# Queueing weight splits and head preparation behind the gates, and taking two experts' maxima from raw weights

## The chip, the cores and the metric

One core of a Trainium2 chip runs the kernel in one launch. The metric is device time in microseconds: the median of the timed runs, and beside it one execution taken by the hardware profiler. The engines named below are TensorE (PE, with its weight loads as PEld), VectorE (DVE), ScalarE (ACT), GpSimd (POOL) and SyncE (SP), whose queue issues all DMAs.

## The reference

Attention with a decay over 4 batches, 8 heads, 576 positions and 64 columns a head; its output is the input of four experts whose outputs are added with normalised weights. All of it is float32.

```python
def _attn_ref(q, k, v, f):
    scores = scale * np.matmul(q, k.transpose(0, 1, 3, 2))
    cum = np.cumsum(np.log(np.clip(f, 0.0001, 1.0)), axis=-1)
    decay = cum[:, :, :, None] - cum[:, :, None, :]
    scores = np.where(causal, -1000000000.0, scores + decay)
    scores = scores - np.max(scores, axis=-1, keepdims=True)
    attn = np.exp(scores)
    attn = attn / (np.sum(attn, axis=-1, keepdims=True) + 1e-09)
    return np.matmul(attn, v)

def _moe_ref(x, domain_probs, w1, w2):      # x: 2304 x 512; w1: 4 x 512 x 1024
    p = domain_probs / (domain_probs.sum(-1, keepdims=True) + 1e-09)
    for e in range(E):
        h = np.maximum(x @ w1[e], 0.0)
        out += p[:, e:e + 1] * (h @ w2[e])
```

## The kernel before

Every float32 product is made of several products of shorter numbers: an operand is split into a high part and the low rest (`hi` and `kl` of a head's q and k, `wh` and `wl` of weights, `gh` and `gl` of the hidden layer), and three of the four combinations are added up in PSUM.

The 2304 tokens are nine chunks of 256. Chunks 0 to 3 are the first 256 positions of each batch (half 0 of the heads), the others the remaining 320 (half 1). After a startup that runs the heads of batch 0, half 0, the experts begin while attention goes on.

The experts' work is a list of 80 **steps**. Weights come in 64 **units** (`w[n % 32]`: 128 hidden columns of `w1` and of `w2`, 512 KB); units 0 to 31 are sweep 0, with chunks 0 to 2 at fp32r, and units 32 to 63 sweep 1, the same weights at f16 for chunks up to 4. A step takes one chunk through two units: `l1` (24 products, L1010), the gate (`gh` by ScalarE at L1023, kept as `self.first`; `gl` by VectorE at L1024, `self.last`), and `l2` (12 products, L1043) with a drain into `acc` (L1070). Step n traces `l1` of n, its gate, then `l2` of n - 1. Chunks 5 to 8 follow in a last stage (from about 630 us, `Big` and `Second`) that reads the split weights back from DRAM (`wd`).

Between these calls `pace` traces attention's work, which the list `asteps` orders and whose costs set how much goes into each quarter step. For head n `head_steps` traces: `prep_v` and `prep` of the next head (`prep_hi`: `hi` on ScalarE L562, `q` on GpSimd L563; `prep_lo`: `kl` L571 and the low rows of `hi` L577 on GpSimd), the loads of the head after that, the score products (L615), minima (L629), exponentials (L644), for half 1 the f16 pair `z` (L713, L714) that a transposing DMA turns into `pt` (L723).

`w_split(n)` is traced at the end of the step whose unit it replaces, six units ahead. In sweep 0 it makes `wh` on ScalarE (L950) and `wl` in two halves (L954), on GpSimd from unit 16 on. In sweep 1 it scales by `wsc`: the first half by ScalarE (L977) and VectorE (L978), the second by GpSimd (L969), ScalarE (L972) and GpSimd (L973); two steps later a DMA writes the pair to `wd`. Raw weights lie in three buffers `wr`, loaded up to three units ahead.

The scale `wsc` of an expert needs the maxima of all its weights ahead of sweep 1. `w_peek` loads each expert's units once more in 16 halves (`pk`, 256 KB, L281), one a step from the step in `PEEK` on, and reduces them two steps later (L284); `w_scale` follows 17 steps after the start and sends the maxima through DRAM (`tops`).

What order the engines' queues have is not that of the text. A scheduler draws it up ahead of time, in a timeline of its own: an instruction may go into its engine's queue ahead of others traced before it, when its data and its buffer are there sooner. On the chip each queue then runs strictly in that order. `tc.issue_after(i)` adds an edge of order alone: what the block traces on i's engine is queued behind i. The helper `behind` uses it with the last step's `gl`.

Of the kernel before, what the change touches and what calls it, by code (L numbers as in the profile page):

```python
# [29 lines left out]
WIDE = (0, 1, 2)  # L30
PEEK = (1, 15, 31, 45)
V_PEEK = 1
# [5 lines left out]
EARLY = (54, 58)  # L38
AHEAD = 4
W_SLOT = (4, 6)  # L40
NEAR = 2
# [37 lines left out]
def fused(ctx: ExitStack, tc: tile.TileContext, qk, v, f, probs, w, out):  # L79
# [413 lines left out]
    class Job:  # L493
# [71 lines left out]
        def prep_lo(self, hh):  # L565
            if hh not in self.kl:
                self.rows(hh)
            wq, wk, ko, qo = self.wq, self.wk, self.ko, self.qo
            r, hi, kl = self.raw[hh], self.hi[hh], self.kl[hh]
            eng = nc.vector if self is jobs[0] else nc.gpsimd  # L570
            eng.tensor_tensor(  # L571
                out=kl[:64, :wk],
                in0=r[:64, ko : ko + wk],
                in1=hi[:64, ko : ko + wk].bitcast(F32),
                op=ALU.subtract,
            )
            eng.tensor_tensor(  # L577
                out=hi[64:128, qo : qo + wq],
                in0=r[64:128, qo : qo + wq],
                in1=hi[64:128, qo : qo + wq].bitcast(F32),  # L580
                op=ALU.subtract,
            )

        def prep(self, hh):
# [291 lines left out]

    zs, pts = [], []
    jobs = []
# [6 lines left out]
    def head_steps(n):  # L885

        st = []
        if FIRST < n < len(heads) and heads[n][1] == 0:
            st.append((0, heads[n][0].prep_v))
        if n + 1 < len(heads):  # L890
            j, hh = heads[n + 1]
            st.append((0, lambda j=j, hh=hh: j.prep(hh)))
        if n + 2 < len(heads):
# [50 lines left out]
    def w_split(n):  # L944
        w_load(n)
        r = wraw.pop(n)
        if n < 32:
            wh[n] = w_p.tile([128, 1024], F32R, tag="wh", name=f"wh{n}")
            wl[n] = w_p.tile([128, 1024], F32R, tag="wl", name=f"wl{n}")
            nc.scalar.activation(out=wh[n], in_=r, func=AF.Copy)  # L950
            eng = nc.vector if n in W_DVE else nc.gpsimd
            for a in (0, 512):
# [664 lines left out]

    used = set()
    for n in range(len(steps) + 1):
# [4 lines left out]
        for e, first_ in enumerate(PEEK):  # L1624
            if 0 <= n - first_ < 16:
                w_peek(e, n - first_)
            if n == first_ + 17:
                a_, b_ = w_scale(e)
                behind(a_)
                at_step(n + 3, b_)  # L1630
        if 0 <= n - V_PEEK < NV:
# [29 lines left out]
        if prev is not None:  # L1661
# [6 lines left out]
            for w0, t in ends.items():  # L1668
                if t is prev:
                    if w0 + 7 < NS:  # L1670
                        w_split(w0 + 6)
                        w_split(w0 + 7)
                    first_units(w0)
        prev = cur

# [89 lines left out]
```

## Time and profile before

| what | us |
|---|---|
| median of 3 runs | 936.33 (935.25 to 938.32) |
| profiled execution | 940.96 |
| its span, first to last instruction | 939.2 |
| TensorE busy | 884.8 |
| VectorE busy | 718.5 |
| ScalarE busy | 567.5 |
| GpSimd busy | 523.7 |

Busy time is the union of an engine's instructions. A value in square brackets behind a row of the timeline is the idle time of the engine before it and what ended it. Times are counted from the span's start.

### The profile page before, as it was taken

How to read it: one execution, taken by the hardware profiler on the slowest of the kernel's cores; microseconds unless marked ns; L12 is line 12 of the kernel's file. 1: busy time of each engine (PE TensorE's matmuls, PEld its weight loads, DVE VectorE, ACT ScalarE, POOL GpSimd, SP SyncE). 2: the span in 40 equal slices, each digit the busy share in tenths (PEclk: the TensorE clock that was granted, in tenths of full speed). 3: DMA queues.
4: the chain of work that ended last, by engine and by line, in shares of the span. 5: the costliest groups of instructions: out<-in, count | busy, mean ns of one | idle time of the engine just before them, and what ended most of it. 6: DMA issues, size and time to landing. Idle time of an engine off the chain costs nothing.

```text
span 939.2 us, 16651 instructions
## 1 busy us (share of the span) xinstructions
PE 884.8 (94%) x5783; PEld 618.9 (66%) x5783; DVE 718.5 (77%) x1458; ACT 567.5 (60%) x1137; POOL 523.7 (56%) x528
## 2 busy tenths in 40 slices
PE   4899999999988999899899999999998999999998
PEld 3699998998755656676566656654455664566547
DVE  5768777786899988789887777576768756786487
ACT  5869766465577667567766676355665345653350
POOL 4666866567533564227752674165778627785060
PEclk9689999999989999999999999999999999999999
DMA  7458855647889799977999698514322423232003
GB/s 263 147 166 308 273 139 172 199 134 235 258 245 184 161 298 217 251 160 160 327 289 183 138 304 219 141 58 146 131 91 79 149 68 120 83 106 75 23 1 91
DMA packets 147508, 159.45 MB, mean 170 GB/s; under 512 B 86148, under 2 KB 107328, under 8 KB 147424
## 3 DMA queue, kind: packets, MB, share of 16 engines
q1 hardware_dynamic: 147424, 158.39, 60.8%
q8 instruction: 45, 0.74, 0.3%
q14 instruction: 39, 0.32, 0.1%
HBM read 117.30 MB, written 21.65 MB: 148 GB/s over the span
## 4 chain that ended last, share of the span: by engine, by line
PE 23%; POOL 13%; DVE 6%; ACT 5%; issue 4%; DMA 2%; POOLq 0%; DVEq 0%; ACTq 0%
PE y L1281 6%; PE m L1281 5%; PE l L1043 5%; POOL s L1341 5%; PE l L1010 4%; POOL wt L1175 4%; POOL wu L1175 2%; DMA wr<-in_w 2%; POOL bs L1207 1%; PE s L615 1%; DVE acc L1070 1%; POOL wr L969 1%; PE o L815 1%; DVE rl L1162 1%; ACT wt L1202 1%
## 5 line engine op out<-in xcount | busy, mean ns | idle before, releaser
L1010 PE MATMUL l<-y,w 128*128 128x256 f16 x1248 | 154.7, 273 | 1.1 <-DVE gl L1024 1.1
L644 ACT ACTIVATE p<-p,nm 128x576 f32<-128x576 f32 (+3 forms) x160 | 95.6, 598 | 72.9 <-DVE nm L629 63.4
L1010 PEld LDWEIGHTS <-w 128*128 128x128 f16 x1248 | 117.7, 98 | 33.3 <-issue 8.9
L1043 PE MATMUL l<-w,gh 128*128 128x512 f16 x408 | 125.1, 390 | 6.9 <-DVE acc L1070 5.3
L714 DVE SCALAR_TENSOR_TENSOR z<-p,rs,z 128x384 f16<-128x384 f32 (+3 forms) x128 | 92.0, 743 | 9.3 <-ACT z L713 7.3
L615 PE MATMUL s<-hi 128*128 128x384 f32 (+1 forms) x192 | 75.5, 397 | 20.6 <-DVE hi L577 8.8
L563 POOL CAST q<-raw 64x320 fp32r<-64x320 f32 (+1 forms) x56 | 26.6, 476 | 120.0 <-PE s L615 79.5
L1070 DVE SCALAR_TENSOR_TENSOR acc<-y,scg,acc 128x256 f32<-128x256 f32 (+1 forms) x164 | 81.1, 515 | 14.9 <-PE y L1281 14.7
L571 POOL TENSOR_TENSOR kl<-raw,hi 64x576 fp32r<-64x576 f32 (+1 forms) x56 | 65.3, 1166 | 39.4 <-ACT hi L562 38.6
L1281 PE MATMUL m<-rh,bs 128*128 128x512 f16 x256 | 86.4, 379 | 0.0
L629 DVE CUSTOM_DVE_ANT_0 p<-s,mask 128x288 f32<-128x288 f32 (+2 forms) x160 | 74.7, 474 | 13.1 <-PE s L615 12.4
L1207 POOL TENSOR_TENSOR bs<-wt,bs 128x512 f16<-128x512 f32 x32 | 38.4, 1202 | 78.2 <-ACT bs L1206 78.0
L1043 PE MATMUL l<-w,gl 128*128 128x512 f16 x204 | 78.5, 390 | 2.0 <-DVE gl L1024 2.0
L969 POOL TENSOR_SCALAR wr<-wr,wsc 128x512 f32<-128x512 f32 x32 | 54.5, 1708 | 36.5 <-DMA wr<-in_w 36.0
L713 ACT ACTIVATE z<-p,rs 128x384 f16<-128x384 f32 (+3 forms) x128 | 69.5, 589 | 6.6 <-DVE rs L675 4.5
L954 POOL TENSOR_TENSOR wl<-wr,wh 128x512 fp32r<-128x512 f32 x48 | 63.1, 1339 | 12.5 <-ACT wh L950 6.9
L1010 PE MATMUL l<-xh,wh 128*128 128x256 f32 x224 | 66.5, 299 | 0.8 <-ACT xh L856 0.8
L1043 PEld LDWEIGHTS <-gh 128*128 128x128 f16 x408 | 37.2, 100 | 44.6 <-issue 14.2
L1024 DVE SCALAR_TENSOR_TENSOR gl<-l,gh 128x512 f16<-128x512 f32 (+1 forms) x80 | 54.7, 684 | 15.0 <-ACT gh L1023 14.4
L1010 PE MATMUL l<-xl,wh 128*128 128x256 f32 x224 | 66.2, 295 | 0.0
L1010 PE MATMUL l<-xh,wl 128*128 128x256 f32 x224 | 65.7, 293 | 0.1
L1281 PE MATMUL m<-rh,bw 128*128 128x512 f16 x191 | 64.4, 379 | 1.4 <-ACT r L1327 1.4
(385 smaller groups left out, 2349.0 us busy)
## 6 DMA issues: line engine op xcount, KB each, us to landing
wr<-in_w SPq DMA_DIRECT2D x90, 512.0 KB
pk<-in_w SPq DMA_DIRECT2D x64, 256.0 KB
wd<-w SPq DMA_DIRECT2D x32, 512.0 KB
raw<-in_qk SPq DMA_DIRECT2D x32, 448.0 KB
bw<-wd SPq DMA_DIRECT2D x32, 256.0 KB
bv<-wd SPq DMA_DIRECT2D x32, 256.0 KB
raw<-in_qk SPq DMA_DIRECT2D x24, 256.0 KB
vp<-in_v SPq DMA_DIRECT2D x10, 512.0 KB
```

Source lines behind the costliest of these rows:

```text
L571: eng.tensor_tensor(out=kl[:64, :wk], in0=r[:64, ko : ko + wk], in1=hi[:64, ko : ko + wk].bitcast(F32), op=ALU.subtract,)
L615: nc.tensor.matmul(out=ps[:, at : at + z - a], lhsT=lhsT, rhs=rhs, start=(m == 0), stop=(m == 1),)
L629: nc.vector.tensor_tensor_reduce(out=pt[:, a:z], in0=ps, in1=mask[:, m0 + a : m0 + z], scale=-0.125, scalar=BIG if n == 0 else nm[:, col : ...
L644: nc.scalar.activation(out=pt[:, :w_], in_=pt[:, :w_], func=AF.Exp, scale=-1.0, bias=self.nmax[hh][:, c : c + 1], accum_out=self.ssum[:, h ...
L713: nc.scalar.activation(out=o[:, 0], in_=x, func=AF.Copy, scale=sc)
L714: nc.vector.scalar_tensor_tensor(out=o[:, 1], in0=x, scalar=sc, in1=o[:, 0], op0=ALU.mult, op1=ALU.subtract)
L954: eng.tensor_tensor(out=wl[n][:, a:z], in0=r[:, a:z], in1=wh[n][:, a:z].bitcast(F32), op=ALU.subtract,)
L969: nc.gpsimd.tensor_scalar(out=r[:, c], in0=r[:, c], scalar1=sc, scalar2=None, op0=ALU.mult)
L1010: nc.tensor.matmul(out=self.l1p[:, fi, :], lhsT=lhsT, rhs=rhs[:, k, :], start=(k == 0 and m == 0), stop=(k == 3 and m == 2),)
L1043: matmul(out=l2[tt], lhsT=lhsT, rhs=rhs, start=(self.ps == 0 and fi == 0 and m == 0), stop=(self.ps == 1 and fi == 1 and m == 2),)
L1070: nc.vector.scalar_tensor_tensor(out=acc[c][:, tt, d0:d1], in0=ps, scalar=sc, in1=acc[c][:, tt, d0:d1], op0=ALU.mult, op1=ALU.add,)
L1281: line.append(nc.tensor.matmul(**args))
```

## The change

Four things change.

- `w_split` is traced inside `paced`, which queues its ScalarE part behind the step's `gh`, its VectorE part behind that step's `gl`, and its GpSimd part behind the last low rows of a head (`lows[-1]`, L577) that were traced so far. The pairs of units that follow a step with `ps` 1 are traced `REST` steps later, by the number of chunks in the sweep.
- `prep` and `prep_v` of the next head are traced inside `held`, the same with the step before.
- Only experts 0 and 1 are still loaded in halves for their maxima. Those of experts 2 and 3 are reduced in `w_split` of units 16 to 31, from the raw unit that lies there, by one reduction over 2 x 512 columns.
- `w_scale` follows at the steps of `SCALE`: 18 and 32 as before for experts 0 and 1, 37 and 42 for 2 and 3 (48 and 62 before).

```diff
-PEEK = (1, 15, 31, 45)
+PEEK = (1, 15)
+SCALE = (18, 32, 37, 42)
+REST = (0, 0, 1, 2, 3)
@@ prep_lo
-            eng.tensor_tensor(
+            i = eng.tensor_tensor(
                 out=hi[64:128, qo : qo + wq],
...
+            if self is not jobs[0]:
+                lows.append(i)
@@ head_steps
-            st.append((0, heads[n][0].prep_v))
+            st.append((0, lambda j=heads[n][0]: held(j.prep_v)))
-            st.append((0, lambda j=j, hh=hh: j.prep(hh)))
+            st.append((0, lambda j=j, hh=hh: held(lambda: j.prep(hh))))
@@ w_split, units below 32
             nc.scalar.activation(out=wh[n], in_=r, func=AF.Copy)
+            if n // 8 >= len(PEEK):
+                nc.vector.tensor_reduce(
+                    out=wmax[:, :, n % 8, n // 8],
+                    in_=r.rearrange("p (k c) -> p k c", k=2),
+                    op=ALU.max, axis=AX.X, apply_absolute_value=True,
+                )
@@ the loop over steps
+    def held(f):
+        if prev is None:
+            f()
+        else:
+            paced(prev, f)
+
+    def paced(t, f):
+        with tc.issue_after(t.first.ins), tc.issue_after(t.last.ins), tc.issue_after(lows[-1].ins):
+            f()
-            if n == first_ + 17:
-                a_, b_ = w_scale(e)
-                behind(a_)
-                at_step(n + 3, b_)
+        if n in SCALE:
+            a_, b_ = w_scale(SCALE.index(n))
+            behind(a_)
+            at_step(n + 3, b_)
...
                     if w0 + 7 < NS:
-                        w_split(w0 + 6)
-                        w_split(w0 + 7)
+                        wait = REST[len(SWEEPS[t.s][t.g // 2])] if t.ps else 0
+                        splits.setdefault(n + wait, []).extend((w0 + 6, w0 + 7))
                     first_units(w0)
+            for m in splits.pop(n, ()):
+                paced(cur or prev, lambda: w_split(m))
```

## Rows read from the trace of the kernel before

**Rows 1.** The page, its head and busy time by engine (share, instructions).

```profile
span 939.2 us, 16651 instructions
PE 884.8 (94%) x5783; PEld 618.9 (66%) x5783; DVE 718.5 (77%) x1458; ACT 567.5 (60%) x1137; POOL 523.7 (56%) x528
```

**Rows 2.** Windows: length, busy PE PEld DVE ACT POOL, granted clock, DMA share, GB/s.

```profile
86.00:206.00 120.00, 117.91 (x800) 108.17 (x800) 88.89 (x225) 78.29 (x177) 79.73 (x91) 0.99 0.60 186
290.00:500.00 210.00, 195.99 (x1422) 133.14 (x1421) 181.22 (x396) 144.92 (x295) 102.17 (x94) 0.98 0.94 231
630.00:939.00 309.00, 297.91 (x1782) 174.01 (x1780) 218.69 (x334) 150.41 (x259) 177.45 (x166) 1.00 0.28 89
```

**Rows 3.** Timeline of PE, 240 to 560 us: what follows an idle piece (start, length).

```profile
264.92 0.61 PE L615 MATMUL s<-hi 128*128 128x288 f32 x1 [4.54 <-DVE nm L629]
...
302.92 1.28 PE L815 MATMUL o<-pt,v 128*64 128x320 f16 x16 [1.95 <-DMA pt<-z]
...
325.62 0.49 PE L1010 MATMUL l<-y,w 128*128 128x256 f16 x3 [1.08 <-DVE gl L1024]
...
334.55 0.50 PE L615 MATMUL s<-hi 128*128 128x512 f32 x1 [1.62 <-DVE ux L203]
...
394.29 2.08 PE L815 MATMUL o<-pt,v 128*64 128x320 f16 x14 [2.89 <-DMA pt<-z]
...
459.01 1.01 PE L1043 MATMUL l<-w,gh 128*128 128x512 f16 x2 [2.68 <-DVE acc L1070]
...
549.97 0.39 PE L1043 MATMUL l<-w,gl 128*128 128x512 f16 x1 [1.98 <-DVE gl L1024]
```

**Rows 4.** Windows around two stretches at half clock, columns as in rows 2.

```profile
264.40:271.20 6.80, 6.28 (x16) 2.89 (x17) 6.74 (x18) 5.78 (x12) 2.93 (x3) 0.50 0.78 161
...
551.10:554.50 3.40, 3.40 (x10) 1.32 (x9) 2.68 (x7) 2.96 (x8) 3.25 (x3) 0.50 1.13 228
```

**Rows 5.** Timeline of ACT around three splits of sweep 1.

```profile
256.24 0.72 ACT L977 ACTIVATE w<-wr,wsc 128x512 f16<-128x512 f32 x1 [4.89 <-DMA wr<-in_w]
...
332.61 0.72 ACT L977 ACTIVATE w<-wr,wsc 128x512 f16<-128x512 f32 x1 [6.59 <-DMA wr<-in_w]
...
436.39 1.93 ACT L977 ACTIVATE w<-wr,wsc 128x512 f16<-128x512 f32 x3
...
440.44 0.60 ACT L1023 ACTIVATE gh<-l 128x512 f16<-128x512 f32 x1
```

**Rows 6.** Waits of ACT: who waited for whom, us in total, times, longest.

```profile
ACT w L977 <- DMA wr<-in_w: 29.0, 10, 6.6
```

**Rows 7.** Timeline of POOL in sweep 0.

```profile
104.51 5.06 POOL L954 TENSOR_TENSOR wl<-wr,wh 128x512 fp32r<-128x512 f32 x4
109.79 2.77 POOL L954 TENSOR_TENSOR wl<-wr,wh 128x512 fp32r<-128x512 f32 x2 [0.21 <-ACT wh L950]
...
117.99 0.74 POOL L577 TENSOR_TENSOR hi<-raw,hi 64x256 fp32r<-64x256 f32 x1
...
200.89 5.23 POOL L954 TENSOR_TENSOR wl<-wr,wh 128x512 fp32r<-128x512 f32 x4 [0.30 <-POOL hi L577]
...
224.98 0.87 POOL L577 TENSOR_TENSOR hi<-raw,hi 64x320 fp32r<-64x320 f32 x1
```

**Rows 8.** Timeline of PE: the first reads of `wl` in steps 9 and 23.

```profile
107.67 0.28 PE L1010 MATMUL l<-xh,wl 128*128 128x256 f32 x1
...
207.63 0.33 PE L1010 MATMUL l<-xh,wl 128*128 128x256 f32 x1
```

**Rows 9.** Groups of DVE, 290 to 500 us: count, busy us, mean ns, idle before.

```profile
L284 DVE TENSOR_REDUCE wmax<-pk 128x1 f32<-128x512 f32 x30 | 20.2, 675 | 4.1 <-DMA pk<-in_w 4.1
```

**Rows 10.** Groups of the whole span, shapes apart: a reduction over 1024 columns.

```profile
L260 DVE TENSOR_REDUCE xmax<-xf 128x1 f32<-128x1024 f32 x6 | 7.2, 1212 | 3.9 <-ACT xf L869 3.9
```

**Rows 11.** One line's instructions: ns at least, median, most; first and last start.

```profile
L978 DVE SCALAR_TENSOR_TENSOR w<-wr,wsc,w x32: 714/752/1985, 208.5 to 583.8; 128x512 f16<-128x512 f32 x32
```

**Rows 12.** DMA packets, 290 to 500 us.

```profile
DMA packets 60090, 48.50 MB, mean 231 GB/s; under 512 B 48100, under 2 KB 48356, under 8 KB 60068
```

More of the change, by code (lines that the diff above doesn't have):

```diff
@@ L874, in out16 @@
                 )
-    zs, pts = [], []
+    zs, pts, lows = [], [], []
     jobs = []
@@ L950, in w_split @@
             nc.scalar.activation(out=wh[n], in_=r, func=AF.Copy)
+            if n // 8 >= len(PEEK):
+                nc.vector.tensor_reduce(
+                    out=wmax[:, :, n % 8, n // 8],
+                    in_=r.rearrange("p (k c) -> p k c", k=2),
+                    op=ALU.max,
+                    axis=AX.X,
+                    apply_absolute_value=True,
+                )
             eng = nc.vector if n in W_DVE else nc.gpsimd
@@ L1616, in fused @@
         w_split(n)
-    used = set()
+    def held(f):
[6 more added lines that the diff above has]
+            f()
+    used, splits = set(), {}
     for n in range(len(steps) + 1):
```

## Prediction

> **What bounds the kernel now.** I read the page first. TensorE is busy for 884.8 us of 939.2 [rows 1], so nothing can be won but the 54 us in which it stands still and the stretches in which it runs at half clock. The table by stage comes next [rows 2]. Most of sweep 0 (86 to 206 us) is full: 117.9 of 120 us, with VectorE at 74% (88.9 of 120) and the DMA engines at 0.60. The thick of sweep 1 (290 to 500 us) has 14.0 us of TensorE idle (210 less 196.0), VectorE at 86% and the DMA engines at 0.94. The stage from 630 us on has 11 us idle in 309 and the change hardly reaches it. So the place to look is sweep 1 and the passage into it.
>
> There I listed TensorE's idle pieces in order of time [rows 3]. Seven are over a microsecond between 240 and 560 us, where the changed work lies. Five end with VectorE: a score product that waits for the row minimum (4.54), a first-layer product that waits for the gate `gl` (1.08), a score product behind the scale chain `ux` (1.62), an l2 product that waits for the drain `acc` (2.68), one that waits for `gl` (1.98). Two end with the transposing DMA `pt<-z` (1.95 and 2.89). After four of the seven the granted clock is at half, 1.2 GHz instead of 2.4: 6.8 us after the largest, 3.4 us each after the pieces at 394, 459 and 550 us (the first and the last of the four stand in [rows 4]). Half clock doubles TensorE's work, so these cost 3.4 us and 1.7 us each.
>
> What made VectorE late? ScalarE's order of time shows it [rows 5]. At 436.39 three weight conversions (L977) run in a row ahead of gate 52 (L1023 at 440.44). By the program they belong later: units 48 and 49 are split in the text behind gate 52, unit 50 behind gate 59. The scheduler moved them up since their data were ready. I counted the gates ahead of every split: units 34 to 63 (30 of 30) run ahead of the gate that the new text puts before them, by three to ten gates. Worse is the conversion at 332.61: ScalarE had stood 6.59 us for its raw weights, with gate, exponentials and head preparation queued behind it. In all, L977 waited 29.0 us in 10 such cases [rows 6]. Behind each, VectorE's half of the split waits too, as at 332 us, where the 1.62 us piece follows.
>
> **Part 1: splits behind gates and spread by REST.** Nothing is added or removed: per unit two conversions on ScalarE, one subtraction on VectorE, two steps on GpSimd, the same DMAs. What moves: in sweep 1 splits come in pairs, each behind its step's `gh` on ScalarE and `gl` on VectorE, and nine of the pairs one to three steps later still. Three conversions take 1.93 us [rows 5], 0.64 each, so a gate that had three or four ahead of it now has none of its own step's. The raw tile has waited steps for its gate, so the 6.6 us kind of wait should go. The loads `wr` and the writes `wd` (two steps after the split) move later with it on SP's queue, past the transposes; the writes are read only in the last stage. Bounds: the five pieces that end with VectorE are 4.54 + 1.08 + 1.62 + 2.68 + 1.98 = 11.9 us, and the half clock after three of them 3.4 + 1.7 + 1.7 = 6.8, together 18.7 us. At the least nothing is won: the same work is then late behind the gate, for the next exponential and drain. I take half, **-9.4 us**: the waits for raw weights (4.89 and 6.59 us of ScalarE ahead of two of the five [rows 5]) go, the work stays.
>
> The price is a shorter lead. Eight pairs (first units 34, 38, 42, 46, 50, 54, 58, 62) are needed by the l1 two steps after their gate, where tens of microseconds lay between. Behind the waiting split stand the next head's `hi` and exponentials on ScalarE. A pair that misses costs about what a late `gl` cost, 1.08 us [rows 3]; none to all eight is 0 to 8.6. I take one, **+1.1 us**, nearest to none, since only the first-half conversions and VectorE's step are needed by l1.
>
> **Part 2: preparation behind gates.** Of the 55 preparations placed by the planner I counted 53 whose `hi` already runs behind the gate now asked for; the two others are at the start. So this edge costs and gains nothing, and the gates themselves hide it. But the same helper queues GpSimd's steps of a *split* behind the last preparation traced (`lows[-1]`), and that order is new. In sweep 0, where GpSimd makes `wl` and the l1 two steps on needs it, it bites [rows 7]. Unit 18's `wl` starts at 104.51 and l1 reads it at 107.67 [rows 8]; it must now follow `hi` of head 19, which ends at 117.99 + 0.74 = 118.73. With a first half of 1.27 (5.06 / 4) that is 120.0, 12.3 us too late. Much of that is the old order's own doing: 5.06 + 2.77 us of `wl` ran ahead of head 19 on GpSimd. Taken off, 4.5 us remain. Bounds: nothing, if attention catches up in TensorE's shadow, and the worst pair, units 30 and 31: `wl` from 200.89 must follow head 33, done at 224.98 + 0.87 = 225.85; with 1.31 for a half, 227.2 against the read at 207.63 is 19.5 us. The shift isn't paid twice, since a preparation once ahead stays ahead. I take **+4.5 us**, by the nearer row.
>
> **Part 3: maxima from the raw units.** 32 `pk` loads of 256 KB and their reductions go, 0.675 us each, 21.6 us of VectorE; 30 of them lie in 290 to 500 us, 20.2 us [rows 9] of the 181.2 there. Added are 16 reductions of 128x1024 in sweep 0. The same form for `xmax` takes 1.21 us [rows 10], so 19.4 us on VectorE, which goes there from 74% to (88.9 + 19.4) / 120 = 90%. In sweep 1 it goes to 77%. The reductions follow the gate of their own step, and the next gate is a step away, which covers two of them (2.4 us); without that cover they would push `gl`. I put their cost into the 4.5 us. The raw buffer is also held until the reduction is done. The DMA engines lose 7.9 MB (30 x 256 KB) of 48.5 MB in 290 to 500 us [rows 12], 16%. The two pieces that end with `pt<-z` are 1.95 + 2.89, with 1.7 of half clock 6.5 us. Bounds nothing and all; I take a third, **-2.2 us**, twice the share of bytes, since the loads also queued ahead of the transposes on SP. `w_scale` of experts 2 and 3 moves from steps 48 and 62 to 37 and 42 with the same instructions; its factors are needed later than either, so nothing.
>
> A row bears on VectorE's half of the split: L978 takes 0.714 at the least, 0.752 in the median and 1.985 at the most [rows 11]; when it meets GpSimd's work it is long. The Trainium skill ("SBUF — State Buffer", section Who interferes with whom) says that a VectorE instruction with two SBUF inputs and a GpSimd instruction that reads SBUF exclude each other for a whole instruction, and that a reduction never does so on trn2. The trace agrees with both (30 `pk` reductions keep to 0.675 in the mean [rows 9]). By that rule pairs that are split at once meet GpSimd's steps of their partner more often; rival B says what it would cost.
>
> **The sum.** -9.4 + 1.1 + 4.5 - 2.2 = -6.0 us. The profiled execution took 940.96 (span 939.2, 1.8 around it), so it would take 935.0. It lies 4.6 above the median of 936.33; the same difference gives **930.3 us**.
>
> **Rivals.** B, *the relief of VectorE is eaten*: the split's L978 meets GpSimd's steps. If the 16 of them in 290 to 500 us go from 0.752 to 1.985, that is 19.7 us, as much as the 20.2 us that leave. VectorE stays at 86% and the gates gain only what the raw waits gave, a quarter (-4.7) instead of half: -4.7 + 1.1 + 4.5 - 2.2 = -1.3, so 935.0, no change that can be told. For it speaks that 752 is a median with a long tail; against it, that the pairs are fewer at a time than the threes of now.
>
> C, *GpSimd ties the experts to attention in sweep 0*: splits wait for the last preparation, that for `q`, and `q` for the score products two heads back; if attention can't run closer behind the text, TensorE stands until it does. The place is 86 to 240 us, the price the worst pair's 19.5 us in place of 4.5: -9.4 + 1.1 + 19.5 - 2.2 = +9.0, so 945.3. It decides the sign from 10.5 us on (9.4 + 2.2 - 1.1). For it: TensorE has no idle time there now, attention lags the text by two to four steps, and VectorE gets fuller. Against it: GpSimd has a third of sweep 0 free (79.7 busy of 120 [rows 2]) and the DMA engines are at 0.60.
>
> **How the numbers follow.** Forecast 0.57, B 0.16, C 0.27. About 0.3% (2.8 us) is what a measurement of this kernel can tell from no change. The forecast is faster, B the same, C slower: 0.57, 0.16 and 0.27. The range runs from all 25.2 us won at the costs taken (-25.2 + 5.6 = -19.6, 916.7) to just over C's 945.3: 916.5 to 946.
>
> **What would show it.** Right: in sweep 1 no ScalarE wait of L977 for `wr` over 2 us, pairs of L977 behind L1023, VectorE near 77% in the stretch of the old 290 to 500 us, fewer stretches at half clock. Wrong: TensorE idle before l1 with GpSimd's `wl` as releaser between 86 and 240 us (C), L978's mean well over its present one (B), or l1 of sweep 1 waiting for L978 (the short lead). If the pieces at `pt<-z` stay, the DMA term was wrong.

## The result, and the profile after

| | before | after |
|---|---|---|
| median of the runs on the same chip, us | 936.83 (935.25 to 938.32) | 928.05 (925.93 to 930.66) |
| ratio, 95% interval | | 0.9911 [0.9883, 0.9938] |
| profiled execution, us (span) | 940.96 (939.2) | 928.71 (926.9) |

The kernel became faster by 8.8 us, 0.9%. 930.3 was forecast. One execution each of experiments 3 and 10 was disturbed (1800 and 5027 us) and is left out of their medians below. The lines have moved with the change: the gate is L1035 and L1036 now (`gh`, `gl`), `l1` L1022, `l2` L1055, its drain L1082, the split of sweep 1 L989, L990 and L981, `wl` of sweep 0 L966, the low rows of `hi` L579. L956 is the new reduction.

The head of the page of after, to lay beside [rows 1]:

```profile
span 926.9 us, 16557 instructions
PE 880.7 (95%) x5783; PEld 619.8 (67%) x5783; DVE 712.2 (77%) x1442; ACT 571.5 (62%) x1137; POOL 527.1 (57%) x528
```

TensorE has the same 5783 products and stands still for 46.2 us instead of 54.4. That is 8.2 us, but the span fell by 12.3, so part of the gain lies in the clock. The windows of after, columns as in [rows 2]:

```profile
60.00:241.00 181.00, 170.47 (x1108) 153.55 (x1107) 144.20 (x335) 117.22 (x261) 109.85 (x124) 0.96 0.59 185
241.00:630.00 389.00, 382.99 (x2773) 263.48 (x2772) 317.95 (x681) 271.01 (x534) 215.27 (x194) 1.00 0.83 211
86.00:206.00 120.00, 112.09 (x719) 100.25 (x718) 95.28 (x223) 74.50 (x171) 76.48 (x86) 0.96 0.56 178
290.00:500.00 210.00, 208.53 (x1558) 143.44 (x1557) 174.17 (x401) 153.98 (x308) 104.83 (x99) 1.00 0.83 201
```

and the first two windows of before:

```profile
60.00:241.00 181.00, 178.10 (x1203) 162.62 (x1201) 137.22 (x330) 120.83 (x267) 121.30 (x133) 0.99 0.67 209
241.00:630.00 389.00, 366.49 (x2614) 246.93 (x2613) 324.94 (x690) 256.00 (x514) 191.83 (x175) 0.98 0.86 213
```

The two stages moved in opposite directions. From 60 to 241 us TensorE is idle for 10.5 us (2.9 before) and does 95 products less in the same time. From 241 to 630 us it is idle for 6.0 us (22.5 before) and does 159 more. In the stretch of [rows 2] from 290 to 500 us 14.0 us of idle time became 1.5.

All idle pieces over a microsecond between 86 and 630 us, from the timeline of PE of after, as in [rows 3]:

```profile
102.24 0.67 PE L795 MATMUL o<-pt,v 128*128 128x256 f32 x4 [1.61 <-DVE xs L838]
...
117.00 0.27 PE L201 MATMUL topx<-ident,xmax 128*1 128x128 f32 x1 [2.14 <-DVE xmax L262]
...
237.80 0.64 PE L1055 MATMUL l<-wh,gh 128*128 128x512 f32 x1 [2.62 <-ACT gh L1035]
...
302.95 1.69 PE L819 MATMUL o<-pt,v 128*64 128x320 f16 x27 [1.39 <-DMA pt<-z]
...
589.98 0.28 PE L1022 MATMUL l<-y,w 128*128 128x256 f16 x1 [1.93 <-ACT w L989]
...
611.03 0.59 PE L1055 MATMUL l<-w,gh 128*128 128x512 f16 x2 [1.26 <-DVE acc L1082]
```

Of the seven pieces of [rows 3] one kind is left between 240 and 560 us, a transposing DMA. Three new ones stand in sweep 0, and within 3 us of each the granted clock falls to half for 3.4 us. A fourth such stretch, from 186.8 us on, has no piece over 0.3 us just ahead of it. The first and the last of the four, in windows of after:

```profile
104.90:108.30 3.40, 3.31 (x16) 3.32 (x16) 2.00 (x5) 1.96 (x6) 3.33 (x6) 0.50 0.58 195
...
238.00:241.40 3.40, 3.40 (x11) 2.61 (x11) 3.34 (x6) 2.30 (x4) 0.00 (x0) 0.50 0.90 169
```

**One account for both.** For each stage I add TensorE's idle time and half of the time that it ran at half clock, counted in short windows one after the other (at half clock half of the time is lost: in before a first-layer product starts 213 ns after the one ahead of it there, 109 ns at the whole clock, medians from 60 to 630 us). Before: 2.9 + 3.4 / 2 = 4.6 us from 60 to 241 us, and 22.5 + 17.1 / 2 = 31.0 us from 241 to 630 us. After: 10.5 + 13.2 / 2, which is 17.2 before rounding, and 6.0 + 0.4 / 2 = 6.2. Sweep 0 lost 12.6, sweep 1 won 24.8, net 12.2 of the 12.3 us of span.

What won sweep 1 is seen in ScalarE's order of time, beside [rows 5]:

```profile
452.38 0.60 ACT L1035 ACTIVATE gh<-l 128x512 f16<-128x512 f32 x1
453.01 1.33 ACT L989 ACTIVATE w<-wr,wsc 128x512 f16<-128x512 f32 x2
454.25 0.61 ACT L984 ACTIVATE w<-wr 128x512 f16<-128x512 f32 x1
454.77 0.71 ACT L648 ACTIVATE p<-p,nm 128x512 f32<-128x512 f32 x1
```

The pair follows its gate at once. The 29.0 us in which L977 waited for raw weights [rows 6] have no row left among ScalarE's waits; L989 never stands for `wr`.

What lost sweep 0 is seen on GpSimd. Its timeline after, beside [rows 7]:

```profile
97.32 0.39 POOL L565 CAST q<-raw 64x256 fp32r<-64x256 f32 x1 [2.02 <-PE s L619]
...
101.98 0.73 POOL L573 TENSOR_TENSOR kl<-raw,hi 64x256 fp32r<-64x256 f32 x1 [4.27 <-ACT hi L564]
102.78 0.80 POOL L579 TENSOR_TENSOR hi<-raw,hi 64x256 fp32r<-64x256 f32 x1
103.66 2.51 POOL L966 TENSOR_TENSOR wl<-wr,wh 128x512 fp32r<-128x512 f32 x2
```

`wl` is queued behind a head preparation that waits 2.02 us for score products and 4.27 us for `hi`, and TensorE stands for `wl` afterwards (0.75 us ahead of 104.98). The wait of GpSimd's `q` for score products is 137.0 us over the span, 86.2 before. Its row among GpSimd's waits:

```profile
POOL q L565 <- PE s L619: 137.0, 32, 10.6
```

### The profile page after: what moved, and what is told of

It is laid out like the page before. It is cut to its first block, busy times and chain, and to the rows that moved or that the text cites. A ratio compares the mean times of both kernels' runs of the same rounds, so it can differ in the third digit from the quotient of the medians.

```text
span 926.9 us, 16557 instructions
## 1 busy us (share of the span) xinstructions
PE 880.7 (95%) x5783; PEld 619.8 (67%) x5783; DVE 712.2 (77%) x1442; ACT 571.5 (62%) x1137; POOL 527.1 (57%) x528
## 4 chain that ended last, share of the span: by engine, by line
PE 42%; POOL 14%; DVE 7%; ACT 5%; issue 4%; DMA 1%; POOLq 0%; DVEq 0%; ACTq 0%
PE l L1022 12%; PE l L1055 12%; PE y L1293 6%; PE m L1293 5%; POOL s L1353 4%; POOL wt L1187 4%; PE s L619 4%; PE o L819 3%; POOL wu L1187 2%; POOL bs L1219 1%; DVE acc L1082 1%; DVE z L718 1%; ACT wt L1214 1%; ACT r L1339 1%; DVE h L1328 1%
## 5 line engine op out<-in xcount | busy, mean ns | idle before, releaser
L1022 PE MATMUL l<-y,w 128*128 128x256 f16 x1248 | 153.6, 273 | 2.7 <-ACT w L989 1.9
L1022 PEld LDWEIGHTS <-w 128*128 128x128 f16 x1248 | 117.4, 98 | 33.5 <-issue 7.1
L1055 PE MATMUL l<-w,gh 128*128 128x512 f16 x408 | 121.4, 380 | 1.3 <-DVE acc L1082 1.3
L718 DVE SCALAR_TENSOR_TENSOR z<-p,rs,z 128x384 f16<-128x384 f32 (+3 forms) x128 | 81.6, 662 | 16.1 <-ACT z L717 14.9
L1082 DVE SCALAR_TENSOR_TENSOR acc<-y,scg,acc 128x256 f32<-128x256 f32 (+1 forms) x164 | 81.1, 515 | 14.9 <-PE y L1293 14.9
L633 DVE CUSTOM_DVE_ANT_0 p<-s,mask 128x288 f32<-128x288 f32 (+2 forms) x160 | 74.7, 474 | 22.4 <-PE s L619 21.8
L1055 PE MATMUL l<-w,gl 128*128 128x512 f16 x204 | 76.7, 379 | 0.0
L1022 PE MATMUL l<-xh,wh 128*128 128x256 f32 x224 | 66.4, 298 | 1.8 <-ACT xh L860 1.6
L1022 PE MATMUL l<-xh,wl 128*128 128x256 f32 x224 | 66.6, 299 | 0.8 <-POOL wl L966 0.7
L966 POOL TENSOR_TENSOR wl<-wr,wh 128x512 fp32r<-128x512 f32 x48 | 63.5, 1351 | 6.7 <-ACT wh L954 4.3
L1022 PE MATMUL l<-xl,wh 128*128 128x256 f32 x224 | 65.8, 295 | 0.5 <-DVE xl L861 0.5
L619 PE MATMUL s<-kl,q 66*128 66x384 f32 (+1 forms) x192 | 62.5, 330 | 3.0 <-DMA kl<-nc 3.0
L1036 DVE SCALAR_TENSOR_TENSOR gl<-l,gh 128x512 f16<-128x512 f32 (+1 forms) x80 | 54.8, 685 | 13.4 <-ACT gh L1035 12.7
L564 ACT ACTIVATE hi<-raw 128x896 fp32r<-128x896 f32 (+1 forms) x56 | 45.2, 808 | 29.2 <-PE s L619 25.3
```

The lines of the kernel that those rows point to most:

```text
L619: nc.tensor.matmul(out=ps[:, at : at + z - a], lhsT=lhsT, rhs=rhs, start=(m == 0), stop=(m == 1),)
L633: nc.vector.tensor_tensor_reduce(out=pt[:, a:z], in0=ps, in1=mask[:, m0 + a : m0 + z], scale=-0.125, scalar=BIG if n == 0 else nm[:, col : ...
L718: nc.vector.scalar_tensor_tensor(out=o[:, 1], in0=x, scalar=sc, in1=o[:, 0], op0=ALU.mult, op1=ALU.subtract)
L966: eng.tensor_tensor(out=wl[n][:, a:z], in0=r[:, a:z], in1=wh[n][:, a:z].bitcast(F32), op=ALU.subtract,)
L1022: nc.tensor.matmul(out=self.l1p[:, fi, :], lhsT=lhsT, rhs=rhs[:, k, :], start=(k == 0 and m == 0), stop=(k == 3 and m == 2),)
L1055: matmul(out=l2[tt], lhsT=lhsT, rhs=rhs, start=(self.ps == 0 and fi == 0 and m == 0), stop=(self.ps == 1 and fi == 1 and m == 2),)
```

## The experiments

Two theories stood against each other for each half of the change: that the gain comes from the gates, or from the maxima; that the price in sweep 0 is GpSimd's new edge (`lows`), or the 16 reductions on VectorE. Every kernel is a new order drawn up by the scheduler, and each median is of three to ten executions, so differences of 2 to 3 us between two of them prove little. Each run's ratio is against the kernel before, run on the same chip (medians 936.15, 936.66 and 936.49 in the three groups of runs).

**1. Without GpSimd's edge.** `paced` orders ScalarE and VectorE only.

```diff
-        with tc.issue_after(t.first.ins), tc.issue_after(t.last.ins), tc.issue_after(lows[-1].ins):
+        with tc.issue_after(t.first.ins), tc.issue_after(t.last.ins):
```

> The changed kernel without the edge that queues GpSimd's part of a split behind the last preparation (lows); the edges behind gh and gl stay. Theory G (GpSimd's new order costs sweep 0, 13.9 us by TensorE's idle and half-clock time up to 241 us): step 28 starts near 241 us as in the kernel before instead of 263, idle time up to 241 us falls from 20.8 to about 12 us, the time from 928 to 914 to 920. Theory R (the new reductions on VectorE cost it): step 28 stays near 263 us and the time within 925 to 931.

Measured: 918.88 us, ratio 0.9821 [0.9769, 0.9872], 9.2 us less than the whole change, and step 28 starts at 236.9 us, as theory G had it. The windows of experiment 1, to lay beside those of after:

```profile
60.00:241.00 181.00, 181.00 (x1244) 165.93 (x1243) 154.20 (x349) 123.44 (x271) 119.32 (x133) 1.00 0.67 207
241.00:630.00 389.00, 375.37 (x2680) 251.27 (x2679) 323.28 (x675) 270.79 (x537) 212.91 (x192) 1.00 0.81 202
```

Its timeline of GpSimd at the place shown of after:

```profile
101.90 2.55 POOL L966 TENSOR_TENSOR wl<-wr,wh 128x512 fp32r<-128x512 f32 x2 [0.73 <-POOL hi L579]
104.40 0.58 POOL L565 CAST q<-raw 64x256 fp32r<-64x256 f32 x1
104.95 2.54 POOL L966 TENSOR_TENSOR wl<-wr,wh 128x512 fp32r<-128x512 f32 x2
...
107.80 0.73 POOL L573 TENSOR_TENSOR kl<-raw,hi 64x256 fp32r<-64x256 f32 x1
```

`wl` runs ahead of `kl` again, TensorE never stands between 60 and 241 us, and the clock is whole. VectorE carries the reductions there too, 154.2 us against 144.2. So the price of sweep 0 is the edge on GpSimd. Not all of the 17.2 us comes back: from 241 to 630 us this kernel has 15.3 (13.6 + 3.4 / 2) where after has 6.2. The edge had pushed the experts back against attention, and sweep 1 repaid 9 of 17. That it did so because transposes and scales were ready sooner fits the pieces: in experiment 1 TensorE stands 2.61 us for a transposing DMA at 284 us and 2.06 us for the scaled `y` at 338 us, in after 1.39 us for one transposing DMA.

**2. The edge for units of sweep 1 and preparations alone.**

```diff
+            for i in (t.first, t.last) + ((lows[-1],) if late_unit else ()):
+                s.enter_context(tc.issue_after(i.ins))
...
-                paced(cur or prev, lambda: w_split(m))
+                paced(cur or prev, lambda: w_split(m), m >= 32)
```

> The changed kernel with the edge behind lows for the splits of sweep 1's units (32 to 63) and for the preparations, but not for the splits of units below 32, where GpSimd makes the wl that the next but one l1 reads. Theory G (the price arises where l1 reads GpSimd's part) says 916 to 922 us, step 28 near 237 us. If the edge costs as much with the units of sweep 1, 924 to 929.

Measured: 923.15 us, 0.9862 [0.9831, 0.9892], between the two ranges. Half of the price (4.9 of 9.2 us) is that of sweep 0's splits: TensorE is busy for 181.0 of 181.0 us from 60 to 241 us, and step 28 starts at 238.2 us. The other 4.3 us come from 241 to 630 us (21.8 in the account below, 15.3 in experiment 1). ScalarE waits for raw units there again, which is a likely cause but not shown to be the only one. The row among its waits:

```profile
ACT w L989 <- DMA wr<-in_w: 9.1, 2, 8.2
```

**3. The reductions made short.** They go over 16 columns of each half instead of 512; the maxima of experts 2 and 3 are then of a part of the weights.

```diff
-                    in_=r.rearrange("p (k c) -> p k c", k=2),
+                    in_=r.rearrange("p (k c) -> p k c", k=2)[:, :, :16],
```

> The changed kernel with the 16 new reductions over 2 x 16 columns instead of 2 x 512, so that the maxima of experts 2 and 3 are those of a part of the weights; all orders and waits stay in the text. It takes about 17 us of VectorE's work out of sweep 0. Theory R: idle time up to 241 us falls by 5 us or more and the time to 918 to 923. Theory G: the time stays within 925 to 931.

Measured: 924.19 us (three executions), 0.9879 [0.9826, 0.9932], an interval that overlaps that of after; the median lies between the two ranges. VectorE lost the work (83.3 us busy from 86 to 206 us, 95.3 in after), yet TensorE's idle time from 60 to 241 us fell only from 10.53 to 9.95 us and the account of sweep 0 from 17.2 to 16.7. The theory that VectorE's load is the price of sweep 0 falls.

**4. The gates alone.** All four experts are loaded for their maxima as before; `paced`, `held`, `REST` and GpSimd's edge stay.

```diff
-PEEK = (1, 15)
+PEEK = (1, 15, 31, 45)
-        if n in SCALE:
-            a_, b_ = w_scale(SCALE.index(n))
+            if n == first_ + 17:
+                a_, b_ = w_scale(e)
```

> The change without its maxima: all four experts' weights are loaded once more and reduced as in the kernel before, w_scale at the old steps; the queueing behind gates and REST stay. By the prediction's terms (splits -9.4, short lead +1.1, GpSimd's order +4.5) about 933 of 936.8. If the gates alone took sweep 1's stalls away (theory S), TensorE's idle time from 290 to 500 us is under 4 us and the time is 928 to 932 even with VectorE's 20 us and the 7.9 MB back. If the maxima were what emptied VectorE and the DMA engines (theory M), idle time there stays over 8 us and the time is 934 or more.

Measured: 927.53 us, 0.9905 [0.9876, 0.9934]: the whole gain of the change without its maxima. The time is just under the range of theory S; TensorE's idle time from 290 to 500 us is 5.4 us, between the 4 of S and the 8 of M.

**5. The maxima alone.** No gates, no `REST`, no edge.

```diff
     def paced(t, f):
-        with tc.issue_after(t.first.ins), tc.issue_after(t.last.ins), tc.issue_after(lows[-1].ins):
-            f()
+        f()
-                        wait = REST[len(SWEEPS[t.s][t.g // 2])] if t.ps else 0
+                        wait = 0
```

> The maxima alone: experts 2 and 3 are reduced from the raw units and w_scale stands at the steps of SCALE, but splits and preparations are queued freely and not delayed, as in the kernel before. Prediction's term: DMA -2.2 and some of the 4.5 us, so 934 to 938, with ScalarE's waits for raw weights still about 29 us in total (theory S). Theory M: idle time from 290 to 500 us halves from 14 us, the time is 928 to 931.

Measured: 942.83 us, 1.0064 [1.0040, 1.0087], slower than before, although 32 loads are gone, and past both ranges. ScalarE's old wait is there still (17.4 us, 29.0 before), and VectorE has a new one. Its row among ScalarE's waits:

```profile
ACT w L989 <- DMA wr<-in_w: 17.4, 9, 5.3
```

Its timeline of VectorE in sweep 0:

```profile
141.08 1.22 DVE L956 TENSOR_REDUCE wmax<-wr 128x2 f32<-128x1024 f32 x1 [6.08 <-DMA wr<-in_w]
142.22 1.27 DVE L478 SCALAR_TENSOR_TENSOR y<-xh,xsc,y 128x1024 f16<-128x1024 f32 x1
143.41 0.74 DVE L1077 TENSOR_SCALAR acc<-l,prob 128x512 f32<-128x512 f32 x1
```

And its timeline of TensorE behind that drain:

```profile
144.21 0.80 PE L1055 MATMUL l<-wh,gh 128*128 128x512 f32 x1 [3.75 <-DVE acc L1077]
```

A reduction that is free to move goes into VectorE's queue ahead of its data. It stands 6.08 us for the raw unit with a drain behind it, and TensorE stands 3.75 us for that drain. In all VectorE waits 9.0 us for such units from 60 to 241 us, 0.8 in the kernel of experiment 1, where the gate holds the reduction back. That is what the new maxima cost without gates in sweep 0, 7.3 us in the account against 4.6 before. But sweep 1 has 28.3 against 31.0, so both stages together are level (35.6 and 35.6), while the medians are 6 us apart. The profiled execution, 940.86 us, is among the fastest of its ten. So the rows show the mechanism, and the 6 us are not explained by them. On ScalarE the conversions of sweep 1 also run up to fifteen gates ahead of the place that the new text gives them, in before up to ten, which may be part of it.

**6. REST taken from the kernel without the edge, and REST alone.** The first has the gates on ScalarE and VectorE with `wait = 0`; the second has the edit of 5 with `REST` left in.

```diff
-                        wait = REST[len(SWEEPS[t.s][t.g // 2])] if t.ps else 0
+                        wait = 0
```

> The changed kernel without lows on GpSimd (918.9 us) and also without REST: both pairs of units are split behind the gates of two steps in a row, none later. Theory O (what matters is that no split runs ahead of its own step's gate on ScalarE and VectorE): 917 to 922 us, ScalarE's waits for raw weights stay under 5 us. Theory P (spreading the pairs matters as much): idle time in 290 to 500 us rises by 4 us or more and the time to 924 to 930; ScalarE's waits for raw weights rise, since the fourth raw unit must be loaded into a buffer that was just freed.

> The change with REST and the maxima, but no queueing behind gates at all. Theory O: splits go ahead of the gates as before, since the scheduler may move them up as soon as a buffer is free but not ahead of where they are traced by much; ScalarE's waits for raw weights stay over 15 us and the time at 936 to 944 (the maxima alone: 942.8). Theory P: 922 to 932.

Measured: 928.84 us, 0.9912 [0.9878, 0.9946] without `REST`, and 942.12, 1.0058 [1.0037, 1.0079] with `REST` but no gate. So `REST` gives 10.0 us behind gates (928.84 less 918.88) and 0.7 us, nothing that can be told, without them. It delays the text of a split, and a split that may move up is moved up: on ScalarE all 32 first-half conversions of sweep 1 stand behind the same gates with `REST` alone as in experiment 5. Gates without `REST` still give 7.8 us (936.66 to 928.84, with the new maxima). Theory P's signs are there: ScalarE waits 4.9 us in 3 cases for raw weights, in experiment 1 never, TensorE's idle time from 290 to 500 us is 11.6 us against 3.2, and from 241 to 630 us there are 23.1 us in the account, 7.8 more than in experiment 1. The pieces lie close together, between 295 and 345 us; four of them from the timeline of PE of the kernel without `REST`:

```profile
295.80 1.69 PE L819 MATMUL o<-pt,v 128*64 128x320 f16 x27 [1.35 <-DMA pt<-z]
...
306.89 1.72 PE L819 MATMUL o<-pt,v 128*64 128x320 f16 x27 [1.16 <-DMA pt<-z]
...
337.78 0.66 PE L619 MATMUL s<-hi 128*128 128x384 f32 x1 [1.91 <-DVE nm L633]
...
343.40 0.61 PE L619 MATMUL s<-hi 128*128 128x288 f32 x1 [2.09 <-DVE nm L633]
```

Pairs bunched behind successive gates would be an explanation, but experiment 10 speaks against it: on ScalarE its splits up to step 43 stand behind the same gates as here, these pieces lie ahead of step 40, and it loses nothing. Which of the delayed pairs is worth the 10.0 us stays open.

**7. The preparation free.** The kernel of experiment 1, with `held` calling its function plainly.

```diff
     def held(f):
-        if prev is None:
-            f()
-        else:
-            paced(prev, f)
+        f()
```

> The changed kernel without lows on GpSimd and with the preparation of heads and of v queued freely, as in the kernel before. The prediction counted 53 of 55 preparations behind their gate already, so it expects 917 to 921 us beside 918.9. If the preparations' gates carry part of the gain, 923 or more.

Measured: 919.48 us, 0.9811 [0.9780, 0.9842], beside 918.88 with it: nothing that can be told.

**8. The maxima without the edge.** The kernel of experiment 1 with the old loads and `w_scale` (the edit of 4), and the kernel of experiment 1 with the 32 loads added back but reduced over 8 columns into a spare place, so that they cost DMA and a buffer and hardly any VectorE.

```diff
-        for e, first_ in enumerate(PEEK):
+        for e, first_ in enumerate(PEEK + (31, 45)):
...
-                out=wmax[:, k, n, e : e + 1], in_=t,
+                out=wmax[:, k, n, e : e + 1] if e < 2 else spare, in_=t if e < 2 else t[:, :8],
```

> The gates of ScalarE and VectorE and REST alone, without lows and with the maxima of all four experts loaded as before. If the maxima are worth nothing (as between the change and the gates alone, 928.1 and 927.5), 917 to 921 us. If VectorE's work counts once GpSimd's order is out of the way, the reductions' place decides: 912 to 916 where those in sweep 0 cost more than those in sweep 1, 922 to 926 where the loads and reductions in sweep 1 do.

> The changed kernel without lows, with the 32 loads of experts 2 and 3 put back but reduced over 8 columns into a spare place only; their maxima still come from the raw units. It measures the 7.9 MB alone: beside 918.9, 922 to 924 if the DMA traffic is what the maxima save in sweep 1 (the old maxima took 923.2), 918 to 920 if it is VectorE's work.

Measured: 923.23 us, 0.9853 [0.9819, 0.9887] with the old maxima, 921.63, 0.9847 [0.9817, 0.9878] with the idle loads. Where nothing else is in the way the new maxima give 4.3 us by the medians, of which the loads are some 2.7. The intervals of the ratios of all three kernels overlap, so the 4.3 is not firm and its division less so. With the edge in place the new maxima give nothing (927.53 and 928.05), without any gate they cost 6.

**9. ScalarE's gate alone.** The kernel of experiment 1 without VectorE's edge.

```diff
-        with tc.issue_after(t.first.ins), tc.issue_after(t.last.ins):
+        with tc.issue_after(t.first.ins):
```

> The changed kernel with the edge behind gh on ScalarE alone; neither VectorE's edge nor GpSimd's. VectorE's half of a split reads what ScalarE wrote, so ScalarE's order should carry the splits of sweep 1: 917 to 923 us. If VectorE's own order matters (the reductions and halves in front of gl), 925 or more.

Measured: 924.57 us, 0.9878 [0.9850, 0.9906], just short of the second range: by the medians VectorE's edge is worth 5.7 us, though the intervals of the two ratios overlap a little. The trace shows at what. In its timeline of VectorE a reduction ahead of its data holds up a gate:

```profile
182.40 1.22 DVE L956 TENSOR_REDUCE wmax<-wr 128x2 f32<-128x1024 f32 x1 [3.15 <-DMA wr<-in_w]
183.54 0.68 DVE L1036 SCALAR_TENSOR_TENSOR gl<-l,gh 128x512 fp32r<-128x512 f32 x1
```

and in its timeline of TensorE a product waits for that gate:

```profile
184.28 0.39 PE L1022 MATMUL l<-xh,wh 128*128 128x256 f32 x1 [1.33 <-DVE gl L1036]
```

Such waits are 9.0 us again from 60 to 241 us, where this kernel's TensorE is idle for 4.6 us and that of experiment 1 never.

**10. Two pairs without REST.** Experiment 1, with `REST` only for groups below 6. The condition goes by the group whose unit is replaced, six units ahead of the pair. So it meets the last two groups of sweep 0, whose pairs are units 32, 33 and 36, 37, and not units 60 and 61, which replace units of group 5.

```diff
-                        wait = REST[len(SWEEPS[t.s][t.g // 2])] if t.ps else 0
+                        wait = REST[len(SWEEPS[t.s][t.g // 2])] if t.ps and t.g < 6 else 0
```

> The changed kernel without lows, and REST no longer for the last groups of the sweep (g 6 and 7), so that units 60 and 61 are split after step 72 instead of 74. The stall of 2.1 us in front of step 76, where l1 waits for the first conversion of unit 60 (L989), should go: 914 to 919 us. If it was only one of two things late there, 918 to 921.

Measured: 916.14 us (three executions), 0.9796 [0.9760, 0.9832], the lowest, and not told apart from experiment 1. Its trace is of the execution of 5027 us, so no times are read from it, but the order of its queues is: on ScalarE the conversions of units 32 and 36 stand behind gates 22 and 28, where experiment 1 has 24 and 30, and that of unit 60 behind gate 74 in both. The expectation was about units 60 and 61, and this kernel does not test it.

**The account of all kernels.** Idle time plus half of the time at half clock, as in the section before, and the medians:

| kernel | 60 to 241 us | 241 to 630 us | median, us |
|---|---|---|---|
| before | 4.6 | 31.0 | 936.8 |
| after | 17.2 | 6.2 | 928.1 |
| 1 no edge on GpSimd | 0.0 | 15.3 | 918.9 |
| 2 edge in sweep 1 | 0.0 | 21.8 | 923.2 |
| 3 short reductions | 16.7 | 7.4 | 924.2 |
| 4 gates alone | 10.1 | 10.9 | 927.5 |
| 5 maxima alone | 7.3 | 28.3 | 942.8 |
| 6 no edge, no REST | 1.9 | 23.1 | 928.8 |
| 6 REST alone | 9.8 | 29.5 | 942.1 |
| 7 no edge, no `held` | 0.0 | 17.5 | 919.5 |
| 8 no edge, old maxima | 0.6 | 19.3 | 923.2 |
| 8 no edge, idle loads | 0.0 | 19.2 | 921.6 |
| 9 no edge on GpSimd, none on VectorE | 4.6 | 15.0 | 924.6 |

The median less the two columns is 903.4 us in the mean, and lies between 900.1 and 907.2 in all thirteen. So the medians spread over 23.9 us and what the account leaves over 7.1: these two stages carry most of what the kernels differ by, and differences of a few microseconds aren't to be read from them. The columns are of one execution each, the medians of several.

## Why the prediction came out

The sign, the places and the size held: 930.3 forecast, 928.05 measured, -6.0 against -8.8. But three terms were each some half of what was measured, and the third offset the other two: by the runs, gates and `REST` gave -13.4, the maxima -4.3, and the edge on GpSimd took 9.2, together -8.5. By stages the sum has -10.5 in sweep 1 and +4.5 in sweep 0, and the account -24.8 and +12.6. The main mechanisms were right; that the total came so near is luck, since errors of both signs cancelled.

**Splits behind gates and REST, -9.4 with 1.1 back.** The runs without GpSimd's edge price this part by itself: with the old maxima it takes 936.7 to 923.2, so -13.4 (experiment 8). The mechanism was the one named: raw waits gone from ScalarE's rows, pairs behind the gate, less half clock from 241 to 630 us (17.1 us before, 3.4 in that kernel, 0.4 in after). The step that was mis-sized is "I take half", with its reason that the same work would be late behind the gate. It mostly wasn't: in that kernel two of TensorE's pieces over a microsecond between 240 and 560 us end with VectorE, 3.5 us together, where five were 11.9. The work does stand behind the gate, as in the rows shown of after, where the pair at 453.01 lets the next exponential start 1.8 us after the gate's end, but TensorE has no piece over a microsecond there. By the account 11.7 us are won in sweep 1 (31.0 to 19.3). The sum took sweep 1 alone, though sweep 0 won too, 4.6 to 0.6 us. Its list of pieces was also one short, since [rows 3] leaves out a wait for the gate `gh` in the timeline of before:

```profile
359.92 1.04 PE L1043 MATMUL l<-w,gh 128*128 128x512 f16 x4 [1.48 <-ACT gh L1023]
```

That `REST` needs the gates (10.0 us with them, 0.7 without) was not in the prediction, which treated them as one part.

**The short lead.** Taken as one pair that misses at 1.1 us. One pair missed, but none of the eight that were counted: it is units 60 and 61. By the program their text moves from step 72 to 74 with `REST`, step 76 reads them, and so they are a ninth pair with a lead of two steps. `l1` of step 76 waits 1.93 us at 589.98 for L989. ScalarE's timeline shows one of the two conversions right behind gate 74, and the other late not by its gate but by what the scheduler put between:

```profile
576.46 0.72 ACT L989 ACTIVATE w<-wr,wsc 128x512 f16<-128x512 f32 x1
...
582.80 0.60 ACT L1035 ACTIVATE gh<-l 128x512 f16<-128x512 f32 x1 [1.18 <-PE l L1022]
587.46 1.33 ACT L1214 ACTIVATE wt<-wt,wsc 128x512 f32<-128x512 f32 x2 [4.06 <-POOL wt L1187]
...
589.22 0.71 ACT L989 ACTIVATE w<-wr,wsc 128x512 f16<-128x512 f32 x1
```

The last stage's first conversion waits 4.06 us for GpSimd with the split behind it. Experiment 1 has the same piece (2.11 us). Whether a longer lead for this pair would win it back was not tested, since experiment 10 left the pair where it was.

**Preparation, nothing.** Right as far as can be told: 0.6 us, inside the noise (experiment 7).

**GpSimd's edge, +4.5.** The mechanism of rival C happened, at the place and through the queue that the prediction named. Step 28 (the first of sweep 1) starts its `l1` at 263.4 instead of 241.1 us, 22.3 us later, past the 19.5 that stood as its bound. The rival's result did not follow, since most of it was a shift between two streams: at step 40 after is level (349.3 against 349.9 us), and attention was ahead meanwhile. The last low rows of the last preparation start 17.7 us sooner. The line's instructions before, with their first and last start:

```profile
L577 POOL TENSOR_TENSOR hi<-raw,hi x56: 723/858/2116, 31.9 to 566.2; 64x320 fp32r<-64x320 f32 x32, 64x256 fp32r<-64x256 f32 x24
```

and after:

```profile
L579 POOL TENSOR_TENSOR hi<-raw,hi x56: 726/859/1231, 32.4 to 548.5; 64x320 fp32r<-64x320 f32 x32, 64x256 fp32r<-64x256 f32 x24
```

What is left is 9.2 us with the new maxima and 4.3 without them (927.53 less 923.23). The term was priced by the shift of one `wl` at 104 us, and it is half of what the edge took; the shift of the whole stage and its repayment were not in the sum. The prediction's own test for C, TensorE idle with `wl` as releaser, shows it once (0.75 us); the other pieces end with `xs`, `xmax` and `gh`, behind attention's work that crowds the same engines. It took experiment 1 to put them down to the edge.

**Reductions on VectorE, inside the 4.5.** Their size was right: 16 of 1.211 us in the mean as in [rows 10], and VectorE at 105.0 of 120 us from 86 to 206 us in experiment 1, 87% where 90% was forecast. Their load costs nothing that shows in sweep 0 (experiment 3). In the old stretch of sweep 1, 290 to 500 us, VectorE did not go to 77% but to 83% (174.2 of 210 us); TensorE did 136 products more there (1558 against 1422). What the prediction missed is their place: a reduction of a raw unit is a new waiter for a DMA on VectorE, and only VectorE's gate keeps it from standing ahead of its data (experiments 5 and 9). The Trainium skill ("SBUF — State Buffer", section Who interferes with whom) says that a reduction does not contend with GpSimd on trn2, and the trace agrees: all 16 take 1.199 to 1.222 us, four of them while GpSimd makes `wl`, beside 1.212 for `xmax`.

**DMA of the maxima, -2.2.** Alone with the gates it is 4.3 us by the medians, of which some 2.7 are the loads, with the edge 0, and without gates it is a loss. The share was nearly right: the bytes from 290 to 500 us fell by 13%, from 48.5 MB in [rows 12] to 42.3, where 16% was forecast, and the DMA engines' busy share from 0.94 to 0.83. Of the two pieces at `pt<-z` one is left (1.39 us). The packets of after in that stretch:

```profile
DMA packets 59531, 42.26 MB, mean 201 GB/s; under 512 B 51020, under 2 KB 51404, under 8 KB 59508
```

The stage accounts say why it does not add up. In sweep 1 the new maxima win 4.7 us with the edge (10.9 to 6.2) and 4.0 without (19.3 to 15.3); in sweep 0 they lose 7.1 with the edge (10.1 to 17.2) and nothing without. Why the two meet in sweep 0 stays open, since short reductions change nothing there.

**Rival B** (L978 meets GpSimd's work) was right as a mechanism and wrong as a price. After has a median of 788 ns where [rows 11] has 752, but experiment 1 has nearly twice that, and is 17 us faster than before. The line's instructions in after:

```profile
L990 DVE SCALAR_TENSOR_TENSOR w<-wr,wsc,w x32: 739/788/1843, 243.0 to 592.7; 128x512 f16<-128x512 f32 x32
```

and in experiment 1:

```profile
L990 DVE SCALAR_TENSOR_TENSOR w<-wr,wsc,w x32: 740/1365/1884, 214.3 to 581.2; 128x512 f16<-128x512 f32 x32
```

So longer steps of the split, where they stand behind the gate, did not decide the time. What stretches them can be read from the overlaps, and here the prediction's "the trace agrees with both" goes too far. In before 22 of the 32 run beside GpSimd's scaling L969 alone, which has one input: 18 of them take 0.741 to 0.789 us, hardly more than the two with GpSimd idle (0.714 and 0.737), and four 0.92 to 1.17. Eight run beside a GpSimd subtraction with two inputs (L571, L577 or L973), seven of them for 1.06 to 1.99 us. In experiment 1 29 of 32 meet such a subtraction.

## What to carry to other kernels

Work whose data the scheduler expects early (weight conversions, maxima) is best queued behind the step's critical instruction on every engine where it could get ahead of it and stand there for a DMA. Delaying its text by some steps besides gave 10.0 us more behind such edges, and nothing that can be told without them, since the scheduler moves it up again. An order edge should lead to the step's own work: one that ties a stream to the last in-order instruction of another stream makes the first wait for everything that the second waits for. Where two streams share TensorE, a delay in one stage can be repaid in the next (here 9 of 17 us), so a price read from one stage is not yet the price in time, and the idle time and the clock of every stage are to be added up before a cause is named. What an edit of order did is seen only in the trace's order of instructions: experiment 10 was written for one pair and moved two others.

## What the runs showed of the hardware that was not expected

The granted clock on record can miss a stretch at half clock; the pace of the products shows it. In the profiled executions of before and after the record has half clock for 23.9 us within the first 60 us, where the change does nothing. Of the eleven experiments whose traces have readable times two show the same, and nine a whole clock there. But the products say otherwise. The same window in before and in experiment 1:

```profile
28.90:52.80 23.90, 20.73 (x82) 17.35 (x82) 17.51 (x47) 17.11 (x44) 18.38 (x23) 0.50 0.62 194
28.90:52.80 23.90, 20.84 (x84) 17.64 (x84) 17.73 (x46) 16.63 (x42) 15.78 (x19) 1.00 0.57 183
```

TensorE does about the same work in it (82 and 84 products), at 0.50 and at 1.00. Two first-layer products in a row from experiment 1's timeline of TensorE, in that window and later:

```profile
44.18 0.41 PE L1022 MATMUL l<-xh,wl 128*128 128x256 f32 x1
44.39 0.41 PE L1022 MATMUL l<-xl,wh 128*128 128x256 f32 x1
...
103.09 0.28 PE L1022 MATMUL l<-xh,wh 128*128 128x256 f32 x1
103.21 0.28 PE L1022 MATMUL l<-xl,wh 128*128 128x256 f32 x1
```

They start 0.21 us apart at 44 us and 0.12 at 103 us. From 28 to 53 us the median is 213 to 214 ns in all thirteen kernels, whatever the record says, as in the later stretches with half clock on record (213 ns); elsewhere from 60 to 630 us it is 109 ns. So the startup ran at half clock in all of them, the columns of the account don't suffer by it, and a difference between the mean clocks of two executions can be one of the record alone.
